# Batch 1's inputs loaded chunk by chunk from GpSimd's queue, together with the weights

One core of one Trainium2 chip. The metric is the device time of one execution in microseconds (us); every number is from fast-state runs.

## The reference

```python
def _attn_ref(q, k, v):                      # each (4, 8, 768, 64), float32
    gamma = 1.0 - 2.0 ** (-5.0 - np.arange(H))
    for t in range(S):                       # S = 768
        state = gamma * state + einsum('bhd,bhe->bhde', k[:, :, t], v[:, :, t])
        y[:, :, t] = scale * einsum('bhd,bhde->bhe', q[:, :, t], state)
# x = y with the heads side by side: (4, 768, 512)
def _moe_ref(x, U, V, w_ch1, w_ch2):         # U 768x32, V 32x768, w1 512x2048, w2 2048x512
    h = x.transpose(0, 2, 1) @ U @ V         # low rank, along the sequence
    u = x + h.transpose(0, 2, 1)
    return u + np.maximum(u @ w_ch1, 0.0) @ w_ch2
```

A retention with decay per head, then a mixer of low rank along the sequence and an MLP along the channels.

## The kernel before

The retention of batches 1 to 3 is computed in six chunks of 128 positions (batch 0 in three of 256): turned k and q give scores, the scores are masked, mixed with v, and a state is carried on. While TensorE works on the MLP of batch b-1, the pieces of batch b's retention are put between its matmuls. `weave` does this: a list of pieces with their costs, and marks (a fraction of the whole cost, a function) that are run when the fraction is reached. Batch 0 has a retention of its own at the start, with nothing to hide behind. GpSimd runs what it is given in the order in which it is emitted (in the trace before, it sat idle 14.9 us for batch 1's k with w2's issues standing behind), so where `weave` emits a preparation, a weight load or a store decides what waits for what there.

```python
    def load_whole(nm, b):                   # k or q of a batch: 4 transfers of 32 partitions, sync queue
        open_in(nm, b)
        src = {"q": q, "k": k}[nm][b]
        for hp in (0, 2, 1, 3):
            nc.sync.dma_start(
                out=turned_in[nm, b][ds(32 * hp, 32)].rearrange("p h c x -> p (h c) x"),
                in_=src[ds(2 * hp, 2)].rearrange("h (c t j) d -> t (h c) (j d)", c=NCK, t=32))

    def feed_more():                         # called after every cast: next loads, in a fixed order
        while n_fed[0] < len(feed) and n_held[0] < RING:
            key, src = feed[n_fed[0]]
            if key[0] == "T" and n_cast[key[1] - 1] < 2 * NCK:
                return                       # k and q of batch b only after the last cast of b-1
            # ... (load_whole k and q, or one natural chunk into the ring)

    def prep_chunk(b, ci):                   # on GpSimd: cast k, scale q, cast k natural, scale v
        prep_turned("k", b, ci)
        prep_turned("q", b, ci)
        if b > 1:
            prep_natural("k", b, ci)
        prep_natural("v", b, ci)

    def store():                             # output tiles go out on GpSimd's queue
        if stores:
            dst, src = stores.pop(0)
            nc.gpsimd.dma_start(out=dst, in_=src)

    # ... after batch 0's retention
    load_u()                                 # U, V, all of w1 on GpSimd's queue
    # ...
    for mb in range(4):
        load_w1(mb)
    gate = rinT.tile([P, 2, NCK, 256], fp32, tag="kin", name="gate")
    nc.gpsimd.tensor_copy(out=gate[:1, 0, 0, :1], in_=w1b[:1, NCB - 1, 511:512])   # holds k and q of batch 1
    # ...
    AT = {1: at(0.39, 0.0625, 0.042), 2: at(0.09, 0.105, 0.05)}     # marks of score and mix
    for b in range(1, B):
        # ...
        for ci in range(NCK):
            s_at, m_at = AT[w][ci]
            marks.append((s_at - 0.6 * step, part(turn_chunk, b, ci)))
            marks.append((s_at, part(score4, b, ci)))
            marks.append((m_at, part(mix4, b, ci)))
            if ci + 3 < NCK:
                marks.append((s_at - 0.55 * step, part(prep_chunk, b, ci + 3)))
            elif b + 1 < B:
                marks.append((m_at + 0.05, part(prep_chunk, b + 1, ci - 3)))
        # ...
        weave(mlp_pieces(b - 1), marks)
```

The w1 loads are four blocks of 512 columns, the w2 loads four blocks of 512 rows, each issued by GpSimd with a cast from float32 to bfloat16. Batches 2 and 3 take u for the MLP through transposing DMAs on the sync queue (`lr_turn` with b > 1), which will matter at the end.

## Time and profile before

| | before |
|---|---|
| time, median of 3 runs | 249.48 us (248.05 to 249.49) |
| span of the profiled execution | 246.0 us, mean granted clock 0.958 |
| TensorE (PE) busy | 218.8 us, 89% |
| first MLP starts / second MLP starts | 31.9 / 98.4 us |

The two starts are the first matmuls of w1 on batch 0 and on batch 1 in the trace; between them lies the stage that the change rearranges. From the second start to the end there are 147.6 us in which PE hardly waits. The prediction shows the other lines.

### The profile page before, as it was taken

How to read it: one execution, taken by the hardware profiler on the slowest of the kernel's cores; microseconds unless marked ns; L12 is line 12 of the kernel's file. 1: busy time of each engine (PE TensorE's matmuls, PEld its weight loads, DVE VectorE, ACT ScalarE, POOL GpSimd, SP SyncE). 2: the span in 40 equal slices, each digit the busy share in tenths (PEclk: the TensorE clock that was granted, in tenths of full speed). 3: DMA queues.
4: the chain of work that ended last, by engine and by line, in shares of the span. 5: the costliest groups of instructions: out<-in, count | busy, mean ns of one | idle time of the engine just before them, and what ended most of it. 6: DMA issues, size and time to landing. Idle time of an engine off the chain costs nothing.

```text
span 246.0 us, 5681 instructions
## 1 busy us (share of the span) xinstructions
PE 218.8 (89%) x2402; PEld 122.3 (50%) x2430; DVE 106.3 (43%) x199; ACT 80.8 (33%) x175; POOL 91.2 (37%) x127
## 2 busy tenths in 40 slices
PE   1588789939779999999999999999999999999992
PEld 1476534536535445445754444447644444584451
DVE  4377334415604642566544525555544342221121
ACT  2465425434412213555532002556410014450000
POOL 2759500319960249971137615820001010000110
PEclk9997779997968999999999999999999999999999
DMA  6993999998999999929999953100011532001212
GB/s 180 290 291 25 143 214 229 211 203 166 198 221 219 250 225 238 257 66 205 210 199 242 241 129 109 21 3 4 0 45 45 150 106 43 3 0 43 86 45 85
DMA packets 64009, 34.69 MB, mean 141 GB/s; under 512 B 39680, under 2 KB 62464, under 8 KB 63984
## 3 DMA queue, kind: packets, MB, share of 16 engines
q1 hardware_dynamic: 56880, 23.66, 46.7%
q0 software_dynamic: 7104, 10.67, 18.7%
q8 instruction: 19, 0.31, 0.6%
q14 instruction: 6, 0.05, 0.1%
HBM read 30.90 MB, written 6.29 MB: 151 GB/s over the span
## 4 chain that ended last, share of the span: by engine, by line
PE 38%; issue 31%; DMA 14%; SPq 8%; POOL 6%; DVE 1%; POOLq 0%; ACT 0%
PE mlp L461 17%; PE mlp L438 14%; DMA qin<-in_q_dram 6%; DMA w2b<-in_moe_w_ch_dram 3%; SPq L111 3%; SPq L158 3%; DMA v<-in_v_dram 3%; DMA w1b<-in_moe_w_ch_dram 3%; POOL out_dram L427 2%; PE r L334 2%; PE r L367 2%; SPq L154 2%; POOL vb L85 1%; PE st L319 1%; PE r L358 1%
## 5 line engine op out<-in xcount | busy, mean ns | idle before, releaser
L438 PE MATMUL mlp<-uT,w1b 128*128 128x256 bf16 (+1 forms) x501 | 90.6, 332 | 1.1 <-issue 0.2
L461 PE MATMUL mlp<-w2b,gT 128*128 128x512 bf16 (+2 forms) x384 | 87.1, 375 | 4.9 <-DMA w2b<-in_moe_w_ch_dram 3.2
L445 ACT ACTIVATE gT<-mlp 128x512 bf16<-128x512 f32 (+1 forms) x88 | 42.7, 490 | 77.0 <-PE mlp L438 76.1
L438 PEld LDWEIGHTS <-w1b 128*128 128x128 bf16 x512 | 49.1, 100 | 33.3 <-issue 3.0
L461 PEld LDWEIGHTS <-gT 128*128 128x128 bf16 x400 | 37.0, 98 | 44.2 <-issue 5.2
L427 POOL DMA_DIRECT2D out_dram<-o x24 | 13.2, 553 | 93.2 <-DVE o L468 93.2
L468 DVE TENSOR_TENSOR o<-mlp,u 128x512 f32<-128x512 f32 (+2 forms) x25 | 16.8, 670 | 48.0 <-PE mlp L461 48.0
L443 DVE TENSOR_SCALAR gT<-mlp 128x512 bf16<-128x512 f32 (+1 forms) x40 | 22.1, 552 | 33.5 <-PE mlp L438 33.5
L340 DVE TENSOR_TENSOR a<-r,mask 128x512 bf16<-128x512 f32 x36 | 23.2, 685 | 19.5 <-PE r L334 17.8
L85 POOL TENSOR_TENSOR qi<-qin,gqT 128x512 bf16<-128x512 f32 x18 | 18.7, 1045 | 19.1 <-DMA qin<-in_q_dram 19.1
L72 ACT ACTIVATE x<-r 128x256 bf16<-128x256 f32 x36 | 11.8, 382 | 29.1 <-PE r L367 28.9
L83 POOL CAST ki<-kin 128x512 bf16<-128x512 f32 x18 | 13.6, 763 | 19.7 <-DMA kin<-in_k_dram 14.9
L85 POOL TENSOR_TENSOR vd<-in,gk 128x512 bf16<-128x512 f32 x18 | 18.7, 1041 | 5.3 <-DMA kin<-in_k_dram 1.8
L402 DVE TENSOR_TENSOR u<-r,x 128x512 bf16<-128x512 f32 (+1 forms) x16 | 14.6, 952 | 6.3 <-issue 3.8
L334 PE MATMUL r<-qT,kT 32*128 32x128 bf16 x288 | 7.7, 226 | 4.5 <-DVE qT L284 4.5
L334 PEld LDWEIGHTS <-kT 32*128 32x128 bf16 x288 | 4.5, 96 | 10.1 <-issue 8.9
L284 DVE STREAM_TRANSPOSE qT<-qi 128x256 f32<-128x256 f32 x18 | 7.3, 406 | 5.1 <-POOL qi L85 5.1
L72 ACT ACTIVATE uT<-r 128x1024 bf16<-128x1024 f32 (+1 forms) x6 | 5.2, 880 | 10.9 <-PE r L416 8.8
L557 DVE TENSOR_TENSOR a<-r,mask 128x1024 bf16<-128x1024 f32 x6 | 7.1, 1216 | 3.9 <-PE r L552 3.9
L530 PE MATMUL mlp<-ident,kb 128*128 128x128 bf16 x24 | 3.1, 312 | 5.4 <-DVE kb L83 5.4
L284 DVE STREAM_TRANSPOSE kT<-ki 128x256 f32<-128x256 f32 x18 | 7.8, 436 | 0.0
L83 POOL CAST kd<-in 128x512 bf16<-128x512 f32 x12 | 7.3, 608 | 0.9 <-POOL qi L85 0.9
(77 smaller groups left out, 135.3 us busy)
## 6 DMA issues: line engine op xcount, KB each, us to landing
out_dram<-o POOLq DMA_DIRECT2D x23, 256.0 KB, 2.9
kin<-in_k_dram SPq DMA_DIRECT2D x12, 384.0 KB, 8.1
qin<-in_q_dram SPq DMA_DIRECT2D x12, 384.0 KB, 13.3
in<-in_v_dram SPq DMA_DIRECT2D x18, 256.0 KB, 5.1
in<-in_k_dram SPq DMA_DIRECT2D x12, 256.0 KB, 5.2
w1b<-in_moe_w_ch_dram POOLq DMA_DIRECT2D x4, 512.0 KB, 9.4
w2b<-in_moe_w_ch_dram POOLq DMA_DIRECT2D x4, 512.0 KB, 8.1
kin<-in_k_dram SPq DMA_DIRECT2D x3, 512.0 KB, 6.3
```

What stands on the lines that cost most here:

```text
L72: nc.scalar.activation(dst, src, AF.Copy)
L83: e.tensor_copy(out=dst, in_=src)
L85: e.tensor_tensor(dst, src, scale, op=ALU.mult)
L284: nc.vector.transpose(out=dst, in_=src)
L334: nc.tensor.matmul(R[hp // 2][:, hp % 2, ts(i, P)], turned("kT", b, ci, i, c, r), turned("qT", b, ci, i, c, r), start=(c == 0), stop=(c == 1))
L340: nc.vector.tensor_tensor(a[:, ds(4 * g, 4)].rearrange("p (n i) m -> p n i m", n=2), R[g][:, :, :256].rearrange("p n (i m) -> p n i m", i= ...
L427: nc.gpsimd.dma_start(out=dst, in_=src)
L438: nc.tensor.matmul(g_p[:, :sz], w1b[:, c, ts(m, P)], uTs[b][:, c, ds(lo, sz)], start=(c == 0), stop=(c == NCB - 1))
L443: nc.vector.tensor_relu(gT[:, m, ds(lo, sz)], g_p[:, :sz])
L445: nc.scalar.activation(gT[:, m, ds(lo, sz)], g_p[:, :sz], AF.Relu)
L461: nc.tensor.matmul(ch[:, :nn], gT[:, m, ts(j, P)], w2b[:, m, ds(n0, nn)], start=(m == 0), stop=(m == NM - 1))
L468: nc.vector.tensor_tensor(o_sb, ch[:, :nn], us[b][:, j, n], op=ALU.add)
```

## The change

The intent: batch 1's k and q come in one go and late, so its retention can start only at 0.39 of the first MLP, and PE waits at three places for loads. Loaded chunk by chunk, in transfers to all 128 partitions, in one queue with the weights and in the order of need, the retention can start at 0.17 and the weights come just when they are used. U and V move to the sync queue so that w1's first block can be issued earlier.

```diff
+    def load_part(ci):
+        # ... (k and q of batch 1 are opened at ci == 0)
+        for nm, src in (("k", k), ("q", q)):
+            for h in range(2):
+                nc.gpsimd.dma_start(
+                    out=turned_in[nm, 1][:, h, ci],
+                    in_=src[1, ds(h, 4, step=2), ts(ci, P)].rearrange(
+                        "h (t j) d -> h t (j d)", j=4))
+        # ... (a tile t of the ring)
+        nc.gpsimd.dma_start(out=t.rearrange("p (h d) -> p h d", h=H),
+                            in_=v[1, :, ts(ci, P)].rearrange("h p d -> p h d"))
# ... U and V as float32 on the sync queue, cast by GpSimd (load_uv, cast_uv)
-    for mb in range(4):
-        load_w1(mb)
-    gate = ...
+    load_w1(0)
     cast_early("v", 2, ("P", 0, 4), ("P", 4, 4))
+    load_w1(1)
+    cast_uv()
# ...
-    (three chunks' k, q and v prepared, w2's four blocks among them)
+    load_part(0)
+    load_w1(2)
+    load_part(1)
+    prep_chunk(1, 0)
+    load_w1(3)
+    load_part(2)
+    prep_chunk(1, 1)
+    load_part(3)
     load_w2(0)
+    prep_chunk(1, 2)
+    load_part(4)
     load_w2(1)
+    load_part(5)
# ...
-    AT = {1: at(0.39, 0.0625, 0.042), ...
-    LR = {1: (0.80, 0.83, 0.88, 0.92), ...
+    AT = {1: at(0.17, 0.075, 0.045), ...
+    LR = {1: (0.66, 0.70, 0.76, 0.82), ...
# ... in the marks of batch 1
                 marks.append((s_at - 0.55 * step, part(prep_chunk, b, ci + 3)))
+                if b == 1 and ci:
+                    marks.append((s_at - 0.5 * step, part(load_w2, ci + 1)))
```

More of the change, by code (lines that the diff above doesn't have):

```diff
@@ L115, in load_whole @@
                                                  c=NCK, t=32))
+    def load_part(ci):
+        if ci == 0:
+            open_in("k", 1)
+            open_in("q", 1)
+        for nm, src in (("k", k), ("q", q)):
[4 more added lines that the diff above has]
+                        "h (t j) d -> h t (j d)", j=4))
+        t = rin.tile([P, 512], fp32, tag="in", name=f"v1_{ci}")
+        n_held[0] += 1
+        ready["v", 1, ci] = t
+        nc.gpsimd.dma_start(out=t.rearrange("p (h d) -> p h d", h=H),
+                            in_=v[1, :, ts(ci, P)].rearrange("h p d -> p h d"))
     def feed_more():
@@ L134, in take @@
         return ready.pop(key)
-    for b in range(1, B):
+    for b in range(2, B):
         feed.append((("T", b), None))
         for ci in range(NCK):
-            if b > 1:
-                feed_natural("k", b, ci)
+            feed_natural("k", b, ci)
             feed_natural("v", b, ci)
@@ L253, in prep_chunk, with load_uv, cast_uv @@
         prep_natural("v", b, ci)
-    def load_u():
-        nc.gpsimd.dma_start(out=Ub, in_=moe_U.rearrange("(j p) r -> p j r", p=P))
-    def load_v(c):
-        nc.gpsimd.dma_start(out=V4[ds(RK * c, RK)], in_=moe_V)
+    uv = {}
+    def load_uv():
+        uv["u"] = rin.tile([P, 512], fp32, tag="in", name="uf")
+        nc.sync.dma_start(out=uv["u"][:, :NCK * RK].rearrange("p (j r) -> p j r", j=NCK),
+                          in_=moe_U.rearrange("(j p) r -> p j r", p=P))
+        for lo, sz in ((0, LO), (LO, S - LO)):
+            t = uv[lo] = rin.tile([P, 512], fp32, tag="in", name=f"vf_{lo}")
+            for c in range(NCB):
+                nc.sync.dma_start(out=t[ds(RK * c, RK), :sz], in_=moe_V[:, ds(lo, sz)])
+    def cast_uv():
+        cast("P", Ub.rearrange("p j r -> p (j r)"), uv["u"][:, :NCK * RK])
+        for lo, sz in ((0, LO), (LO, S - LO)):
+            cast("P", V4[:, ds(lo, sz)], uv[lo][:, :sz])
     def load_w1(mb):
@@ L651 @@
     score_early(2)
-    load_u()
+    load_uv()
+    load_w1(0)
     cast_early("v", 2, ("P", 0, 4), ("P", 4, 4))
-    for c in range(NCB):
-        load_v(c)
-    for mb in range(4):
-        load_w1(mb)
-    gate = rinT.tile([P, 2, NCK, 256], fp32, tag="kin", name="gate")
-    nc.gpsimd.tensor_copy(out=gate[:1, 0, 0, :1], in_=w1b[:1, NCB - 1, 511:512])
+    load_w1(1)
+    cast_uv()
     state_early(3)
@@ L695 @@
     feed_more()
-    for ci in range(3):
-        prep_turned("k", 1, ci)
-    for ci in range(3):
-        prep_turned("q", 1, ci)
-    prep_natural("v", 1, 0)
+    load_part(0)
[6 more added lines that the diff above has]
+    load_part(3)
     load_w2(0)
+    prep_chunk(1, 2)
+    load_part(4)
     load_w2(1)
-    prep_natural("v", 1, 1)
-    prep_natural("v", 1, 2)
-    load_w2(2)
-    load_w2(3)
+    load_part(5)
     def at(b0, dc, dm):
         return [(b0 + dc * ci, b0 + dc * ci + dm) for ci in range(NCK)]
-    AT = {1: at(0.39, 0.0625, 0.042), 2: at(0.09, 0.105, 0.05)}
-    LR = {1: (0.80, 0.83, 0.88, 0.92), 2: (0.71, 0.75, 0.83, 0.89)}
+    AT = {1: at(0.17, 0.075, 0.045), 2: at(0.09, 0.105, 0.05)}
+    LR = {1: (0.66, 0.70, 0.76, 0.82), 2: (0.71, 0.75, 0.83, 0.89)}
     for b in range(1, B):
```

## The prediction

> **What bounds the kernel now.** First the slices of the page: TensorE (PE) is nearly full from slice 13 on, so only the first 75 us can give time. (One digit is 6.15 us; `DMA` at 9 is 90% or more.)
>
> ```profile
> PE   1588789939779999999999999999999999999992
> POOL 2759500319960249971137615820001010000110
> PEclk9997779997968999999999999999999999999999
> DMA  6993999998999999929999953100011532001212
> ```
>
> The DMA row is full from slice 4 to 11 (25 to 74 us) while PE has holes in slices 8 to 11. The chain of waits, in order of time, says what the holes wait for:
>
> ```profile
> 25.02 6.23 DMA w1b<-in_moe_w_ch_dram
> ...
> 31.37 0.20 POOL gate L659
> ...
> 39.83 14.35 DMA qin<-in_q_dram
> 54.24 0.10 issue
> 54.34 1.05 POOL qi L85
> ...
> 61.87 7.99 DMA w2b<-in_moe_w_ch_dram
> ```
>
> Three loads in turn: w1's first block, then batch 1's q (held until w1's first block by the gate), then w2. The waits of PE put sizes on them (total, times, longest, us):
>
> ```profile
> PE r L334 <- DVE qT L284: 4.5, 1, 4.5
> PE mlp L461 <- DMA w2b<-in_moe_w_ch_dram: 3.2, 2, 1.7
> PE mlp L673 <- DMA w1b<-in_moe_w_ch_dram: 2.1, 1, 2.1
> ```
>
> That is 9.8 us of idleness. It has a tail, seen in windows of 5 us (PE busy first, then PEld, DVE, ACT, POOL; PEclk is the granted clock):
>
> ```profile
> 50.00:55.00 5.00, 1.46 (x16) 1.26 (x14) 0.30 (x1) 1.60 (x4) 0.66 (x1) 1.00 1.15 198
> 55.00:60.00 5.00, 4.09 (x57) 3.04 (x57) 3.15 (x7) 1.21 (x4) 4.99 (x7) 0.66 0.93 195
> 70.00:75.00 5.00, 4.78 (x51) 2.19 (x51) 0.17 (x1) 0.95 (x3) 1.49 (x2) 0.50 1.16 225
> ```
>
> After each hole PE runs at half clock: the trace's clock records have 0.5 at 31.5-34.9, 55.4-58.8 and 69.1-75.9. Half of these 3.4, 3.4 and about 6 busy us is lost: 1.7 + 1.7 + 3.0. The whole prize is so 9.8 + 6.4 = some 16 us; a PE that never waited after 29 us would end near 234. The question is how much of it the new order really delivers.
>
> [...] landings of the 32-partition k/q loads follow each other by 1.88 us for 393 KB (209 GB/s), while the 128-partition loads of the first 15 us run at 290 GB/s. [...] Trace: w1 blocks land every 2.5 us alone, but the fourth, beside the k loads, 5.1 us after the third. [...] The trace shows its price by number of rows: 0.50 us for V (32 rows), 0.55 for an output tile (128), 0.79 for a w1 block (512), 1.00 for U (768). [...]
>
> **The change part by part.**
>
> *Start.* w1's block 0 is issued at 20.0 instead of 25.0 and, at 5 to 6 us to landing, is there by 26; PE needs it at 29.2. U and V go through the sync queue as float32 and are cast on POOL (three casts, about 1.4 us), in time for 26.4. The 2.1 us wait goes, but the uT evictions end only at 30.4, so the MLP starts near 30.2 instead of 31.9: **-1.7 us**, and the half clock at 31.5 goes: **-1.7**.
>
> *What POOL pays.* The timeline of POOL before:
>
> ```profile
> 25.02 3.05 POOL L262 DMA_DIRECT2D w1b<-in_moe_w_ch_dram  x4
> 31.37 0.19 POOL L659 CAST gate<-w1b 1x1 f32<-1x1 bf16 x1 [3.30 <-DMA w1b<-in_moe_w_ch_dram]
> 46.44 2.10 POOL L83 CAST ki<-kin 128x512 bf16<-128x512 f32 x3 [14.88 <-DMA kin<-in_k_dram]
> ...
> 63.41 0.79 POOL L83 CAST ki<-kin 128x512 bf16<-128x512 f32 x1
> 64.11 1.06 POOL L85 TENSOR_TENSOR qi<-qin,gqT 128x512 bf16<-128x512 f32 x1
> 65.12 1.05 POOL L85 TENSOR_TENSOR vd<-in,gk 128x512 bf16<-128x512 f32 x1
> 66.10 0.76 POOL L83 CAST ki<-kin 128x512 bf16<-128x512 f32 x1
> ```
>
> One chunk's preparation repeats every 2.69 us (63.41 to 66.10). Between 31.6 and 57 POOL did almost nothing. Now each chunk's load is issued there: four k/q transfers of 128 rows at 0.55 and one v of 1024 rows, which the line through the four prices above puts at 1.15: **3.35 us a chunk, 20.1 for six**. From 20.0 to the last w2 issue POOL owes: 8 weight issues x 0.78 = 6.2; casts of batch 0's v 2.1; U and V 1.4; parts 20.1; preparations 6 x 2.69 = 16.1. Sum 46, so the last issue ends at **66** even if POOL never waits. The transfers need less: 6 x (1.8 for k/q at 290 GB/s + 1.15 for v) + 8 x 2.5 = 38 us. POOL, not DMA, becomes the bound of this stage.
>
> *Order on POOL* (starts, adding these up): part 0 25.2, part 1 29.4, prep 0 32.8, part 2 36.2, prep 1 39.6, part 3 42.3, w2 block 0 45.6, prep 2 46.4, part 4 49.1, w2 block 1 52.4, part 5 53.2, prep 3 56.6, prep 4 59.3, w2 block 2 62.0, prep 5 62.7, w2 block 3 65.4.
>
> *Need on PE.* The up and down projections cost 41.5 us a batch; score c is marked at 0.17 + 0.075c of it; a chunk costs PE 1.56 us (natural k 0.43, score 0.33, query 0.23, mix 0.34, state 0.23), the low-rank rest 1.0. From 30.2: scores at 38.3, 42.9, 47.6, 52.3, 56.9, 61.6. Chunk 0 waits about 1.1 for the 2.36 us of additions that empty the same PSUM banks, marked just before. Chunk 3 is the bad one: needed at 53.4, but its q is cast by 58.3 and turned by 58.75: **a stall of 5.4 us**, with half clock after it (1.7). w2's last block, needed at about 71.5, lands near 72.3 beside batch 2's loads: about 1 us more. So the first MLP would end near 30.2 + 41.5 + 1.0 + 8.7 (chunks) + 1.7 (low-rank of batch 1) + 9.2 = **92.3, against 98.4 before: -6.1**, and the kernel at 243.4, if nothing waits later.
>
> *Given back later.* Batch 2's k and q load only after batch 1's last casts, now 63.5 instead of 69.55, still in 32-partition transfers. And the preparation marks of batch 2 moved with batch 1's marks: two chunks of it now stand ahead of the first output store in POOL's order (0.49 and 0.565 of the work; the store at 0.583), the third ahead of the second store. Before, two stores came first:
>
> ```profile
> 75.82 0.61 POOL L427 DMA_DIRECT2D out_dram<-o  x1 [4.33 <-DVE o L468]
> 82.30 0.56 POOL L427 DMA_DIRECT2D out_dram<-o  x1 [5.87 <-DVE o L468]
> 88.42 1.04 POOL L85 TENSOR_TENSOR qi<-qin,gqT 128x512 bf16<-128x512 f32 x1 [4.79 <-DMA qin<-in_q_dram]
> ...
> 95.04 0.57 POOL L427 DMA_DIRECT2D out_dram<-o  x1
> ```
>
> In the trace q's last landing is 18.7 us after the first k issue; that puts it at 82 to 84 now, and the chunks' natural rows 2.4 and 4.2 us later. Prep of chunks 0 and 1 then ends at 89 to 90.5; store 0 issues there and lands some 3.6 us later (95.04 to 98.59 before), at 93 to 94.5. There are three output buffers, so the fourth output tile, done by PE near 85, waits for that landing, its PSUM bank stays taken, and VectorE (in order) behind it; stores 1 and 2 land at 96.5 to 98.5. With three banks PE stops at its next MLP: first piece at 93 to 95, second only at 97 to 98.7, third at 98 to 99.6, against 100.5 before. Gain left there: **1 to 2.5 us**, and the new idleness likely costs some half clock (0 to 2). Sum: 249.5 - 1.7 (middle) + 1 = about 248.5.
>
> **The rivals.** *A, PE keeps the gain:* if part issues on POOL are cheaper than the line says (2.6 instead of 3.35 gives 4.5 us), or batch 2's loads run quicker, store 0 lands before 92 and the end is 240 to 244. For it: the marks look tuned to such a supply. Against it: U's 1.00 us for 768 rows. *B, the stores take it all:* as worked out, 247 to 251. *C, new transfers are poor:* k/q now have a source of 4 heads x 32 rows; if few engines work on each, or GpSimd issues must wait for earlier landings (the weights' issues do carry such waits, eight transfers back), POOL slips by 4 us or more and the time is 252 to 257. *D, hidden anyway:* the DMA was full before, so order cannot help; but at equal DMA time four more chunks would be done when w2's last block comes, which speaks against no effect within the first MLP.
>
> **Range and chances.** B in the middle, A a quarter, C a tenth: 248.5 us, 8 in 10 within 242 to 254.5; faster by over 2% (below 244.5) 0.25, within 2% 0.64, slower 0.11.
>
> **What would show it.** POOL busy without a gap from 20 to about 66, v issues near 1.15 us; no PE wait on w1b; MLP start near 30; a wait of about 5 us for chunk 3's qT on VectorE; the wait on w2b at most 1.5; then a wait of VectorE's output tile on a DMA store near 85 to 95 and a PE hole at 92 to 98; from 100 us on nothing changed. Wrong if the parts issue faster, if PE stalls on w2b for long, or if the first output store is issued before 88 us.

## The result, and the profile after

The kernel became slower: **255.87 us** median (254.98 to 257.43, 4 runs) against 248.76 (247.42 to 249.49, 4 runs) of the kernel before. Ratios here are the mean time of one kernel's fast runs over that of the other's of the same rounds, so not quite the ratio of the quoted medians: 1.0299, 95% interval 1.0223 to 1.0375. The profiled run is the slowest of the four (257.43 us, span 255.6), that of the kernel before took 247.82; 9.6 us of span are to be explained, while the medians differ by 7.1.

| profiled execution | before | after |
|---|---|---|
| span, mean granted clock | 246.0 us, 0.958 | 255.6 us, 0.95 |
| POOL (GpSimd) busy | 91.2 us | 111.7 us |
| first MLP starts | 31.9 | 28.7 |
| second MLP starts | 98.4 | 107.3 |
| from there to the end | 147.6 | 148.3 |

So the loss lies almost wholly between the two starts: 66.5 us became 78.6, which is 12.1 more, less 3.2 won at the start: 8.9 of the 9.6.

The slices of the page, after (one digit is now 6.39 us):

```profile
PE   1588987681990899999999999999999999999992
POOL 2758799999910169295204931960000110000110
DMA  6998799999799999614999965300002343001112
```

POOL is full from slice 5 to 10 (32 to 70 us; its timeline below shows it at work from 27 on), much as predicted, and PE has its deepest hole in slice 12 (77 to 83 us), after POOL has become idle. The waits of PE (total, times, longest, us) say for what:

```profile
PE mlp L486 <- DMA w2b<-in_moe_w_ch_dram: 7.4, 1, 7.4
PE mlp L321 <- DVE kT L309: 5.7, 1, 5.7
PE mlp L463 <- DMA w1b<-in_moe_w_ch_dram: 4.1, 2, 2.4
```

With 1.4 us for turned q, that is 18.6 us of waiting after the MLP's start, against 7.7 before (4.5 for q and 3.2 for w2; the 2.1 for w1 lay ahead of the start). These 10.9 us are most of the 12.1. The wait for w2 is the largest. The chain of waits, in order of time (start, length, what):

```profile
38.34 8.88 DMA w1b<-in_moe_w_ch_dram
...
70.35 13.58 DMA w2b<-in_moe_w_ch_dram
```

The last w2 block took 13.6 us from its issue to its landing. The timeline of the sync engine's queue, and the DMA queues in 72.5 to 75 us (packets, MB, share of the 16 engines' time), show beside what:

```profile
68.47 2.02 SPq L111 DMA_DIRECT2D kin<-in_k_dram  x4
```

```profile
q1 hardware_dynamic: 544, 0.54, 111.3%
```

Batch 2's k (4 x 384 KB) had been issued on the sync queue 1.9 us before the block, as batch 1's last casts were done, with q behind it. In these 2.5 us GpSimd's queue (q0; q1 is the sync engine's) has no line at all: w2's last block moved not one packet. From 75 to 77.5 it got 49 packets, beside 474 of q1, and only then an equal share (297 beside 293). The block before it, issued at 66.86 with no load of the sync queue ahead, needed 5.7 us.

GpSimd's own timeline shows why it was issued so late:

```profile
27.03 0.40 POOL L83 CAST V<-vf 128x256 bf16<-128x256 f32 x1 [2.35 <-DMA vf<-in_moe_V_dram]
27.51 1.43 POOL L123 DMA_DIRECT2D kin<-in_k_dram  x2
28.93 1.35 POOL L123 DMA_DIRECT2D qin<-in_q_dram  x2
30.27 0.94 POOL L130 DMA_DIRECT2D v<-in_v_dram  x1
```

A part cost 1.43 + 1.35 + 0.94 = 3.7 us of issuing, and the first part began 2.3 us late, because the cast of V's last columns (in brackets: 2.35 us idle, ended by V's load) stood ahead of it.

The two longest holes (5.7 and 7.4 us) have half clock at and after them again; the waits for w1 (2.4 us at most) do not, the clock was 1.00 in 36 to 40 us. Windows of 5 us, columns as in the prediction (PE busy first, the clock third from the end):

```profile
60.00:65.00 5.00, 1.82 (x24) 1.17 (x25) 1.69 (x4) 0.60 (x1) 5.00 (x7) 0.50 1.15 201
85.00:90.00 5.00, 4.78 (x34) 1.93 (x34) 0.69 (x1) 0.66 (x2) 0.00 (x0) 0.51 1.22 199
```

The clock records have 0.5 from 59.2 to 69.4 and from 79.7 to 89.9. Eight matmuls of w2 took 3.57 us at 0.5 (from 83.98) and 1.90 us at 1.0 (from 92.19). PE was busy 6.2 and 5.7 us in the two stretches, so, counted as in the prediction, half of the busy time, an estimated 6.0 us were lost. Counted in the same way, the kernel before lost 5.9 (the prediction has 6.4). Half clock is therefore not what made the difference; only the gain of some 4.7 us that the prediction saw in it did not come.

### The profile page after: what moved, and what is told of

Same layout as the page of the kernel before. It is cut to its first block, busy times and chain, and to the rows that moved or that the text cites. A ratio compares the mean times of both kernels' runs of the same rounds, so it can differ in the third digit from the quotient of the medians.

```text
span 255.6 us, 5707 instructions
## 1 busy us (share of the span) xinstructions
PE 218.4 (85%) x2401; PEld 121.5 (48%) x2430; DVE 107.4 (42%) x199; ACT 80.7 (32%) x175; POOL 111.7 (44%) x154
## 4 chain that ended last, share of the span: by engine, by line
PE 33%; issue 30%; DMA 17%; POOL 12%; SPq 5%; DVE 0%; ACT 0%; POOLq 0%; ACTq 0%
PE mlp L486 16%; PE mlp L463 12%; DMA w2b<-in_moe_w_ch_dram 5%; DMA w1b<-in_moe_w_ch_dram 3%; DMA kin<-in_k_dram 3%; DMA v<-in_v_dram 3%; SPq L173 3%; POOL out_dram L452 2%; SPq L169 2%; DMA vf<-in_moe_V_dram 2%; POOL vd L85 2%; POOL kin L123 2%; POOL qin L123 2%; POOL v L130 1%; PE r L392 1%
## 5 line engine op out<-in xcount | busy, mean ns | idle before, releaser
L486 PEld LDWEIGHTS <-gT 128*128 128x128 bf16 x400 | 37.8, 99 | 49.7 <-issue 10.4
L493 DVE TENSOR_TENSOR o<-mlp,u 128x512 f32<-128x512 f32 (+2 forms) x25 | 16.8, 670 | 57.1 <-PE mlp L486 50.2
L85 POOL TENSOR_TENSOR vd<-in,gk 128x512 bf16<-128x512 f32 x12 | 12.5, 1039 | 6.1 <-PE r L392 3.5
L123 POOL DMA_DIRECT2D kin<-in_k_dram x12 | 8.6, 717 | 0.1
L123 POOL DMA_DIRECT2D qin<-in_q_dram x12 | 8.1, 678 | 0.6 <-DMA w1b<-in_moe_w_ch_dram 0.6
```

Of the source, the lines that this page charges most:

```text
L85: e.tensor_tensor(dst, src, scale, op=ALU.mult)
L123: nc.gpsimd.dma_start(out=turned_in[nm, 1][:, h, ci], in_=src[1, ds(h, 4, step=2), ts(ci, P)].rearrange("h (t j) d -> h t (j d)", j=4))
L486: nc.tensor.matmul(ch[:, :nn], gT[:, m, ts(j, P)], w2b[:, m, ds(n0, nn)], start=(m == 0), stop=(m == NM - 1))
L493: nc.vector.tensor_tensor(o_sb, ch[:, :nn], us[b][:, j, n], op=ALU.add)
```

## The experiments

The theory after the trace: three things cost the time, each by where an instruction stands in GpSimd's order. w2's last blocks are issued so late that they stand behind batch 2's loads; chunk 3's preparation stands too late (5.7 us); and with both mended, the output stores would be the next to wait, as predicted and, after this change, hidden by PE's own lateness. Rivals: the new transfers are slow in themselves, or the sum of the transfers bounds the stage wherever they stand. Each of the thirteen kernels is compared with runs of the kernel before on the same chip; all are correct. A run over 1.5% above the fastest of its kernel counts as slow and is left out: 4 of 20 in both_stores_first and in w1_first, 1 of 4 in t2_held, 2 of 4 in chunks32. Every profile is of a fast run.

### w2_early

w2's blocks 2 and 3 issued right behind part 5.

```diff
     load_part(5)
+    load_w2(2)
+    load_w2(3)
-                if b == 1 and ci:
-                    marks.append((s_at - 0.5 * step, part(load_w2, ci + 1)))
```

> Edit: w2's blocks 2 and 3 are issued right after part 5, before the preparations of chunks 3 to 5, so before batch 2's loads are released. Theory (order on POOL; the last w2 block starves behind batch 2's k and q loads on the sync queue): the PE wait on w2b goes from 7.4 us to under 1, block 3 lands near 74 instead of 83.9, the wait for chunk 3 grows by the two issues (5.7 to about 7.3), and the time falls by 6 to 9 us, to 247 to 250; the gain may end at the output stores that stand behind batch 2's preparation. Rival (the GpSimd queue's transfers are simply slow): block 3 still lands after 80, and the time stays within 1% of 255.9.

Measured: 253.14 us (251.04 to 254.51), ratio 1.0194 [1.0137, 1.0251]. The interval allows no verdict at 2%, and the expected 247 to 250 us were missed. PE's wait for w2 is gone: the last block is issued at 61.75, 6.9 us ahead of batch 2's loads (68.63), and lands at 73.26. The wait for chunk 3 is 7.3 us, and VectorE now waits 13.5 us for output stores to free a tile (longest 10.2). The second MLP starts at 99.1 instead of 107.3, and PE waits 2.0 us for the output tiles, 0.9 of it just ahead of that start and 1.1 behind it. The spans differ by 6.4 us and the medians by only 2.7: the profiled run is the fastest of its four, and that of the changed kernel the slowest of its four.

### prep3_first

Chunk 3's preparation put ahead of w2's second block and part 5.

```diff
     load_part(4)
+    prep_chunk(1, 3)
     load_w2(1)
-                marks.append((s_at - 0.55 * step, part(prep_chunk, b, ci + 3)))
+                if b > 1 or ci:
+                    marks.append((s_at - 0.55 * step, part(prep_chunk, b, ci + 3)))
```

> Edit: chunk 3's preparation moved ahead of w2 block 1 and part 5 on POOL, nothing else. Theory: the wait for chunk 3's kT falls from 5.7 us to about 2, but the last w2 block is issued as late as before and lands near 84, so the PE wait on w2b grows by as much and the time stays within 1% of 255.9. Rival (chunk 3's late preparation is what costs): the time falls by 4 us or more.

Measured: 257.58 us (257.11 to 258.12), ratio 1.0388 [1.0367, 1.0409]. The wait for chunk 3 falls from 5.7 to 1.2 us, and that for w2 rises from 7.4 to 12.5. PE came to w2's last block earlier and waited there: the block landed at 84.86, against 83.94 in the changed kernel. What ends this stage is the landing of that block, not the sum of the holes.

### both_moved

Both edits together.

```diff
     load_part(4)
+    prep_chunk(1, 3)
     load_w2(1)
     load_part(5)
+    load_w2(2)
+    load_w2(3)
# ... and both marks taken away
```

> Edit: both moves. Theory: the holes at chunk 3 and at w2 go (left: about 2 and 3 us at chunks 3 and 4), the first MLP would end near 93, but the first output store stands behind two preparations of batch 2 and is issued near 94, so VectorE's fourth output tile waits for it and PE for a PSUM bank: the time is 248 to 251, little better than with w2 alone. Rival (the stores do not matter): 241 to 244.

Measured: 254.65 us (253.64 to 256.22), ratio 1.0268 [1.0224, 1.0311]. The expected time was missed. The wait for chunk 3 is down to 2.6 us, but the one for w2 is not gone: the last block, issued at 64.60, was 5.7 us ahead of batch 2's loads (70.34), yet stood behind its own queue (the block before it landed at 73.90) and then beside those loads. It landed at 78.73, after 14.1 us, and PE waited 4.7 us. The expected new wait is there, in VectorE's timeline (idle before it, and what ended it, in brackets):

```profile
102.27 0.69 DVE L493 TENSOR_TENSOR o<-mlp,u 128x512 f32<-128x512 f32 x1 [10.53 <-DMA out_dram<-o]
```

Store 0 was issued only at 98.04, behind two preparations of batch 2 that waited for their loads, and landed at 102.15. This is the wait on a store that the prediction had placed at 85 to 95. PE was then busy only 3.30 and 3.47 us of the 5 in 100 to 105 and 105 to 110.

### both_stores_first

Both edits, and batch 2's first three preparations marked behind the stores.

```diff
-                marks.append((m_at + 0.05, part(prep_chunk, b + 1, ci - 3)))
+                marks.append((m_at + 0.05 if b > 1 else (0.76, 0.80, 0.88)[ci - 3],
+                              part(prep_chunk, b + 1, ci - 3)))
```

> Edit: both moves, and batch 2's first three preparations marked at 0.76, 0.80 and 0.88 of the first MLP's work, so that three output stores stand ahead of them. Theory: no wait of an output tile on a store, first MLP ends near 93, time 240 to 244. Rival (the stores do not matter): the same time as with both moves alone.

Measured: 248.06 us (246.19 to 249.68, 16 fast runs), ratio 0.9985 [0.9955, 1.0015]. No output tile waits for a store, the second MLP starts at 97.7. So with these three positions mended the kernel is back at the time of the kernel before; but a gain of the kind hoped for is not there, and not even that of the start alone (start_only, ratio 0.9886): about 1% is still lost to something else. PE still waits 3.8 us for turned k, 3.0 for w1, 2.3 for w2 and 1.7 for q.

### stores_first_only

The stores' edit alone.

```diff
-                marks.append((m_at + 0.05, part(prep_chunk, b + 1, ci - 3)))
+                marks.append((m_at + 0.05 if b > 1 else (0.76, 0.80, 0.88)[ci - 3],
+                              part(prep_chunk, b + 1, ci - 3)))
```

> Edit: the changed kernel with batch 2's first three preparations marked behind the third output store, nothing else. Theory (the late w2 block hides the stores in the changed kernel: PE reaches the end of the first MLP only at 107 us, when the first stores have nearly landed): within 1% of 255.9. Rival (the stores' place costs the changed kernel by itself): 3 us or more faster.

Measured: 256.04 us (255.07 to 257.05), ratio 1.0309 [1.0269, 1.035]: no gain, as the theory said. In the changed kernel the stores' delay lies beside the wait for w2, and is worth nothing until that is mended.

### t2_held

The stores' edit, and batch 2's loads held back by a gate until w2's last block has landed.

```diff
+    def load_w2_gated(j):
+        load_w2(j)
+        if j == 3:
+            gate = rinT.tile([P, 2, NCK, 256], fp32, tag="kin", name="gate")
+            nc.gpsimd.tensor_copy(out=gate[:1, 0, 0, :1], in_=w2b[:1, NM - 1, DM - 1:DM])
+            w2_in.append(True)
+            feed_more()
-            if key[0] == "T" and n_cast[key[1] - 1] < 2 * NCK:
+            if key[0] == "T" and (n_cast[key[1] - 1] < 2 * NCK or not w2_in):
```

> Edit: the changed kernel with the stores first as above, and batch 2's k and q loads held until w2's last block has landed (a gate tile written on POOL from that block). w2's blocks are issued as late as in the changed kernel. Theory (w2's last block is late because the sync queue's loads of batch 2 go ahead of it, not because it is issued late): it lands some 6 us after its issue at 70.4, near 76 instead of 83.9, the PE wait on w2b falls from 7.4 us to under 1.5, time 244 to 248. Rival (it is late by its own queue): it still lands after 81 and the time stays above 252.

Measured: 253.14 us (251.61 to 253.46, 3 fast runs), ratio 1.0176 [1.0133, 1.0219]. The mechanism is shown: issued at nearly the same time as in the changed kernel (71.47 against 70.35), with the sync queue empty, the block lands in 5.7 us instead of 13.6. The chain of waits has:

```profile
71.47 5.72 DMA w2b<-in_moe_w_ch_dram
```

The queues in 71.5 to 77.5 us have GpSimd's alone, with 864 packets. PE's wait for w2 is 0.8 us and the second MLP starts at 97.8. The expected time was still missed: batch 2's loads start 9 us later, and a wait comes up one batch further on, at the third MLP:

```profile
PE mlp L473 <- DMA uT<-u: 4.4, 1, 4.4
```

From the second start to the end are now 153.5 us instead of 148.3.

### start_only

The kernel before with only the start changed: U and V on the sync queue, w1 issued from 20 us on.

```diff
-    load_u()
+    load_uv()
+    load_w1(0)
# ... (V's four loads go)
-    for mb in range(4):
-        load_w1(mb)
+    load_w1(1)
+    cast_uv()
+    load_w1(2)
+    load_w1(3)
```

> Edit: the kernel before with the change's first part alone: U and V through the sync queue as float32 and cast on POOL, w1's blocks issued from 20 us on; batch 1's loads, preparations and marks as before. Theory (the start of the change is worth having, the loss is all in what follows): PE has no wait for w1's first block, the MLP starts near 29 instead of 31.9, the gate opens near 27, so the wait for chunk 0's q shrinks too; time 3 to 5 us below before. Rival (casting U and V on POOL or their late landing costs as much as it gives): within 1% of before.

Measured: 245.85 us (244.89 to 246.0), ratio 0.9886 [0.9855, 0.9917]. The MLP starts at 30.0 instead of 31.9 and no wait for w1 is left. This part of the change is a gain of 1.1%, near the 3.4 us (1.7 and 1.7) that the prediction gave it, but below the 3 to 5 us expected here: the wait for q, expected to shrink, is 5.5 us against 4.5. The rest of the change costs some 10 us on top of it (255.9 against 245.9, of different chips).

### after_hw

The changed kernel with the 30 loads of batch 1 issued by the sync engine, in the same shapes.

```diff
-                nc.gpsimd.dma_start(
+                nc.sync.dma_start(
                     out=turned_in[nm, 1][:, h, ci],
# ... the same for v
```

> Edit: the changed kernel with batch 1's thirty loads issued on the sync queue instead of on GpSimd, shapes, places and marks kept. Theory (POOL's issue time, 3.7 us a chunk, is what makes chunk 3 late): POOL has 22 us less to do, the wait for chunk 3's kT falls from 5.7 us to under 1; but without one queue's order the loads can overtake w1's blocks 2 and 3, whose waits (4.1 us) may grow. Time 246 to 253. Rival (the 128-partition chunk loads are slow by themselves, whoever issues them): chunk 3 still waits over 3 us, time above 253.

Measured: 268.86 us (267.8 to 270.63), ratio 1.0832 [1.0781, 1.0883]. The theory's expectation was far off, the rival's was right (chunk 3 waits 1.5 and 2.8 us): relieving GpSimd of the issues does not pay in this shape. PE's largest wait is w2 again, 12.6 us in two: the last block, issued at 82.10, 4.5 us after batch 2's loads (77.61), took 13.5 us to land. The DMA engines were busy 0.34 of their time in 45 to 50 us (86 GB/s), against 0.90 (162 GB/s) in the changed kernel, and at 57.8 us the fifth part was begun on the sync queue, where the changed kernel issued its sixth at that time. Of the 16 engines' time in 45 to 50 us the sync queue's packets took 23.1% and GpSimd's 10.8%. How many engines worked on one of these loads, which ones, and why the share was so low, no run here shows.

### w1_first

both_stores_first with w1's blocks 2 and 3 issued ahead of part 0.

```diff
     load_w1(1)
+    load_w1(2)
+    load_w1(3)
     cast_uv()
# ...
     load_part(0)
-    load_w1(2)
     load_part(1)
     prep_chunk(1, 0)
-    load_w1(3)
```

> Edit: on the kernel with both moves and the stores first, w1's blocks 2 and 3 are issued before batch 1's first part instead of between the parts. Theory (w1's blocks came late because they stood behind the parts in POOL's issue and in the queue): the wait for w1 (3.0 us there, 4.1 in the changed kernel) goes to under 0.5; all six parts land about 2 us later (the two issues of 1.6 us move ahead, the transfers' sum is the same), so chunks 0 to 2 may wait up to 2 us; time 244 to 248, 1 to 4 us below the 248.7 of that kernel. Rival (the sum of transfers bounds this stage): the waits at the chunks grow by as much, time within 1 us.

Measured: 248.70 us (247.67 to 250.46, 16 fast runs), ratio 1.0021 [1.0, 1.0043], no gain on both_stores_first. The 3.0 us for w1 are gone, and other waits have taken their place (3.1 for gT on VectorE, 2.5 for u, 2.4 for turned k). Moving a load ahead in the one queue moved the wait to another place here; this speaks for the rival, that in this form the supply as a whole is too slow.

### chunks32

The order chunk by chunk kept, the shape and issuer given back: 32-partition loads on the sync queue, as in the kernel before; w1 all first, a gate on its first block, w2 between the preparations, stores first.

```diff
-            for h in range(2):
-                nc.gpsimd.dma_start(
-                    out=turned_in[nm, 1][:, h, ci],
+            for hp in (0, 2, 1, 3):
+                nc.sync.dma_start(
+                    out=turned_in[nm, 1][ds(32 * hp, 32), :, ci],
+                    in_=src[1, ds(2 * hp, 2), ts(ci, P)].rearrange(
+                        "h (t j) d -> t h (j d)", t=32))
# ... v on the sync queue too; all six load_part first, then prep and load_w2 in turn
```

> Edit: chunk by chunk and early, but issued by the sync queue in the old 32-partition form (four transfers of 64 KB for k, four for q, one for v a chunk), gated behind w1's first block; all of w1 issued before; POOL has only the preparations and w2; marks of the changed kernel, stores first. Theory (order of need is right, GpSimd as the issuer was the flaw, and heads as the outermost of four rows was the flaw of the sync-queue run): no POOL-made wait at chunk 3, w2's last block lands before 68, first MLP ends near 90, time 238 to 243. Rival (the stage is bound by the sum of transfers, whoever issues and in whatever order): PE waits of 8 us or more in sum before 75 us, time 245 or more.

Measured: only two fast runs, 241.29 and 244.91 us (the other two took 246.41 and 246.43), ratio 0.9808 [0.972, 0.9897]. The runs spread too much for a verdict at 2%. PE's waits in the stage are 3.0 for q, 1.9 for v, 1.4 for u and 1.1 for k; none for w1.

### chunks32_w2first

chunks32 with w2's four blocks issued together behind the first preparation.

```diff
     prep_chunk(1, 0)
+    for j in range(4):
+        load_w2(j)
     prep_chunk(1, 1)
# ... and the four single load_w2 taken away
```

> Edit: as chunks32, but w2's four blocks are issued right after the first chunk's preparation. Theory (a GpSimd-issued block moves only when the sync queue's loads leave room): the chunks are hardly later (under 1.5 us), w2's blocks land earlier than in chunks32, time within 1.5 us of it. Rival (both queues share evenly): the chunks land up to 8 us later, chunk waits grow, time 3 us or more above chunks32.

Measured: **244.11 us** (243.79 to 244.18), ratio 0.985 [0.9828, 0.9871], faster than both kernels: 1.5% below the kernel before, clear of noise but under the 2% of a verdict. Of this the start by itself gives 1.1% (start_only), so the order chunk by chunk adds little. GpSimd's timeline:

```profile
39.73 3.04 POOL L293 DMA_DIRECT2D w2b<-in_moe_w_ch_dram  x4
...
58.24 1.04 POOL L85 TENSOR_TENSOR vd<-v,gk 128x512 bf16<-128x512 f32 x1 [5.65 <-DMA v<-in_v_dram]
```

The blocks land at 48.3 to 59.1 us, well ahead of need, and now chunk 2's v comes late: GpSimd waits 5.65 us for it and takes it up at 58.24, against 51.91 in chunks32. The DMA queues in 50 to 55 us:

```profile
q0 software_dynamic: 777, 0.77, 90.9%
q1 hardware_dynamic: 778, 0.21, 30.3%
```

The two queues moved nearly the same number of packets, 777 and 778. So the theory's mechanism, that a GpSimd-issued block moves only when the sync queue leaves room, was wrong in this stretch, and the rival's even sharing was right; the time came out as the theory said all the same. The second MLP starts at 94.8, 3.6 us earlier than in the kernel before, and nothing is given back later: the span is 242.0 against 246.0.

### marks_by_landing

chunks32_w2first with the marks set to the landings seen there.

```diff
-    AT = {1: at(0.17, 0.075, 0.045), ...
-    LR = {1: (0.66, 0.70, 0.76, 0.82), ...
+    AT = {1: [(s, s + 0.045) for s in (0.17, 0.26, 0.60, 0.67, 0.74, 0.84)], ...
+    LR = {1: (0.90, 0.93, 0.955, 0.98), ...
```

> Edit: as chunks32_w2first, with batch 1's marks set by where its trace shows the rows landing: chunks 0 and 1 early (0.17, 0.26), chunks 2 to 5 at 0.60, 0.67, 0.74 and 0.84, the low-rank steps at 0.90 to 0.98. Theory (what is left of the loss there is PE standing still for chunks marked before their rows land: 5.0 us in two waits at chunk 2, and the 10 us of half clock after them): those waits fall below 1 us in sum, the half clock goes, time 237 to 242. Rival (the loads' sum bounds the stage wherever the marks stand): the waits only move, to w2 or to the start of the second MLP, time within 1.5 us of 244.1.

Measured: 244.52 us (244.04 to 244.9), ratio 0.9863 [0.9826, 0.9899]; no gain. The waits for chunks are gone, and a new one has come. The waits of PE and of VectorE:

```profile
PE r L384 <- DVE a L366: 5.1, 2, 4.7
```

```profile
DVE o L494 <- DMA out_dram<-o: 8.8, 1, 8.8
```

GpSimd was held in the sixth chunk's preparation until 72 us, so the first three stores were issued together at 72.35, 4 us after batch 2's loads (68.43), and took over 9 us to land. It is the wait of w2's last block again, with another transfer.

### stores_ahead

marks_by_landing with that preparation behind the three stores.

```diff
-                    marks.append((s_at - 0.55 * step, part(prep_chunk, b, ci + 3)))
+                    marks.append((0.755 if (b, ci) == (1, 2) else s_at - 0.55 * step,
+                                  part(prep_chunk, b, ci + 3)))
```

> The kernel of marks_by_landing with one thing moved: the preparation of batch 1's sixth chunk stands behind the first three output stores of batch 0 in GpSimd's order instead of ahead of them. Theory (the stores were late only because GpSimd was held in that preparation till 72 us, and queued behind batch 2's loads): stores 0 to 2 are issued before 70 us and land within about 4 us, VectorE's wait of 8.8 us on a store and TensorE's hole of 4.7 us at 83 us go, no half clock in 82 to 89: 237 to 241 us, 1.5 to 3 per cent under the kernel before's 248. Rival (the transfers' sum bounds the stage, wherever the stores stand): the wait comes up again at the sixth chunk or at w2, within 1.5 us of 244.5.

Measured: 248.39 us (247.34 to 250.11, 12 runs), ratio 1.0009 [0.9979, 1.0038]. Both theories missed. The stores, issued at 66.88, 68.02 and 73.04, land within 3 us, the hole at 83 us is gone (its line is no longer among PE's waits), and the second MLP starts at 89.4, 6 us earlier than in marks_by_landing. But the sixth chunk's casts are what lets batch 2's loads go; those start at 74.37 instead of 68.43, batch 3's at 111.78 instead of 106.95, and the transposes of u for the third MLP stand behind these in the sync queue. The timeline of that queue, and PE's waits:

```profile
74.37 2.93 SPq L111 DMA_DIRECT2D kin<-in_k_dram  x4
...
140.27 15.93 SPq L436 DMA_TRANSPOSE uT<-u  x6
```

```profile
PE mlp L464 <- DMA uT<-u: 8.6, 1, 8.6
```

From the second start to the end are 158.9 us instead of 146.9. All that was won in the first MLP, and more, is paid at the third, in this wait and in the half clock after it (143.7 to 153.9).

## Why the prediction was wrong, point by point

- *Start*: right, and better. The MLP started at 28.7 against 30.2 foreseen and 31.9 before, and start_only shows the gain by itself (2.7 us between the medians).
- *What POOL pays*: right in kind, 5 us short in size. The last w2 issue stood at 70.35 instead of 65.4. Three terms make that up: V's cast held the first part by 2.3; a part cost 3.7 instead of 3.35, times six 2.1 (the k and q issues 0.68 to 0.72 each, not 0.55; v's 0.93, not 1.15); and a wait of 0.6 for w1's landing inside a part.
- *"No PE wait on w1b"*: wrong. Blocks 2 and 3 landed at 39.61 and 47.22, each behind parts in the same queue, and PE waited 4.1 us. w1_first shows that this wait can be removed, and that the time then does not change.
- *Chunk 3's stall of 5.4 us*: right, 5.7 measured, but the close match is partly luck: PE came to it at 57.1 instead of 53.4 (w1's waits), and its turned k and q were ready at 62.8 and 63.7 instead of 58.75 (GpSimd's slip). prep3_first shows it was worth nothing by itself.
- ***The step that failed***: "w2's last block, needed at about 71.5, lands near 72.3 beside batch 2's loads: about 1 us more." It landed at 83.94 and PE waited 7.4 us. The prediction, too, had the block issued 1.9 us after batch 2's loads (65.4 and 63.5; measured 70.35 and 68.47). It let the two share the engines, with 6.9 us from issue to landing. In the trace the loads issued first went first, the block got nothing in 72.5 to 75 us and little in the next 2.5, and landed after 13.6. So the landing came 11.6 us later than foreseen: 5.0 by GpSimd's slip, 6.7 by the time behind the loads. PE, itself 5 us late, waited 7.4 instead of 1. t2_held shows it with the queue empty (5.7 us to landing), w2_early with an earlier issue (no wait). Why the block got no turn at first, while in chunks32_w2first the two queues moved 777 and 778 packets side by side, is not shown.
- *Half clock*: the prediction let only one piece of it stay (1.7 us); the two holes drew two long ones, about 6.0.
- The first MLP was to end at 92.3; the second one started at 107.3. The terms: start -1.5, w1 +4.1, w2 +6.4, chunk 3 +0.3, half clock +4.3, together +13.6 of 15.0. The rest, 1.4, is not assigned.
- *Given back later*: the hole behind the output stores did not show: VectorE waited 6.9 us for stores, but PE, late by then, made no hole of it. stores_first_only shows that it was worth nothing here, w2_early and both_moved that it is real (waits of 10.2 and 10.5 us on VectorE) once w2's blocks are issued earlier; both_moved and both_stores_first, which differ in the stores alone, are 6.6 us apart.
- *The rivals*: C had the right size (252 to 257, by a slip of GpSimd of 4 us or more) with a chance of a tenth; its reasons were half right. The issues were dearer, but the transfers themselves were not poor on GpSimd's queue (162 to 217 GB/s in 35 to 50 us, weights included, though the prediction had reckoned with 290 for k and q); in the same shape on the sync queue they were (after_hw, 86 GB/s in 45 to 50 us).

What stays open: why no order went clearly below 244 us (a single run of chunks32 took 241.29). Loading batch 2 early makes w2 or the stores wait (7.4 us on PE in the changed kernel, 8.8 on VectorE in marks_by_landing); loading it late makes the third MLP wait (4.4 us in t2_held, 8.6 in stores_ahead). That these trade against each other is shown; that the sum of the transfers is the limit is only argued, since no run made it smaller.

## What to carry to other kernels

When a transfer's issue moves, ask what has been issued on any queue by then, not only what stands ahead of it on its own: a block issued 1.9 us after a batch of large loads took 13.6 us instead of 5.7. Issuing it earlier is not enough when its own queue is full: in both_moved it was issued 5.7 us ahead of those loads and took 14.1. Moving many loads to an engine that also prepares data makes that engine's order the schedule of everything behind it: here six parts of 3.7 us each stood on GpSimd, and w2's last issue came at 70.35 us instead of 62.67. So add up its issue prices from the very shapes, and leave the last transfer that must beat the next batch a slack larger than the error of that sum. And when a hole is closed, follow what it had held back: here the same loads, stores and transposes met again one batch later, so judge a repair by the end and not by its own stage.

## What the traces show of the queues and of issue prices

- In two stretches with both queues under way they moved nearly equal numbers of packets: 297 of GpSimd's queue beside 293 of the sync queue in 77.5 to 80 us, 777 beside 778 in 50 to 55 us of chunks32_w2first. Ahead of the first of them, in the changed kernel, the packets of the queue whose transfers had been issued first went first: 0 packets of GpSimd's queue beside 544 of the sync queue in 72.5 to 75 us, 49 beside 474 in the next 2.5. In 70 to 71 us it was the other way round: 186 packets of GpSimd's queue and none of the sync queue, whose loads had been issued from 68.47 on. In the kernel before, w2's blocks, issued first, moved 406 packets in 69 to 71 us and batch 2's k, issued from 69.55 on, one. What a transfer paid behind another queue's backlog: w2's block 13.6 us against 5.7, three output stores of marks_by_landing over 9 us against 3.6 for one of the kernel before (95.04 to 98.59).
- The price of one GpSimd issue by shape (the prediction's prices by rows are such prices): 0.50 us for 32 rows, 0.55 for an output tile of 128 rows, 0.68 to 0.72 for k and q of 128 rows out of 4 heads, 0.79 for a weight block of 512 rows with a cast, 0.93 for v of 1024 rows of 256 B, 1.00 for U of 768 rows of 128 B with a cast. The pattern counts beside the number of rows (128 rows cost 0.55 or 0.68 to 0.72, and 1024 rows less than 768), so a line through the rows missed both ways.
- The same 30 loads issued by the sync engine instead of GpSimd made the whole kernel 268.9 us against 255.9, with the DMA engines busy 0.34 of their time in 45 to 50 us against 0.90.
